# Value products and logits ahead of the output products behind the attention, and the last convolution on VectorE alone

## Chip, cores and metric

One core of a Trainium2 chip runs the whole program. The metric is device time in microseconds (us), the median of the runs shown. The profile is one further execution, and its times are counted from its first instruction.

## What is computed

The reference chains three blocks on 4 sequences of 576 rows (2304 rows, 512 channels). Cut to what matters:

```python
# 1 linear attention, 8 heads of 64, features exp(+-(x @ w_phi - max|x @ w_phi|))
num = einsum(q_p, einsum(k_p, v)); x = num / (einsum(q_p, sum(k_p)) + 1e-6)
# 2 gated convolution over the rows
gate = sigmoid(sum(conv_w[k] * shift(x, 4 - k) for k in range(5)))
y = (gate * (x @ w_val)) @ w_out
# 3 sticky top-1 mixture of 8 experts
logits = y @ w_gate; local = y @ w_local
e[s] = argmax(logits[s]) if s == 0 or sigmoid(local[s]) < 0.5 else e[s - 1]
out[s] = softmax(logits[s])[e[s]] * (relu(y[s] @ w1[e[s]]) @ w2[e[s]])
```

## The kernel before

The rows are cut into 18 tiles of 128 and 9 groups of 256. Each engine runs its instructions in the order in which the program has them. A scheduler sets that order from the order of the code and its own estimate of times; instructions given to `pin` (`keep_in_program_order`) keep the order of the code on their engine.

**Attention and mixing (to about 265 us).** `run` walks the k tiles and then the q tiles. For each finished group g, `push_mix` queues the work that follows: two pairs of value products (`val`, L356, tile `vps`, 24 products a pair, three for each fp32 product because both operands are split into a high and a low part), two tiles of output products of the group four back (`ypart`, `ymm`, L495, tile `yps`, 12 products a tile), and the logits (`lgt`, L395). `fill` takes from this queue between the attention's steps. `conv` (L228) makes the gate of a group, channel block by channel block (c = 0 to 3): one ScalarE product and four VectorE multiply-adds (`tap`, tile `acc`), then a tanh on ScalarE (`gp`). Block 3 is made on GpSimd instead (`pool`, L250, tile `p`). `val` ends in `gv = (gate + 1) * vps` on VectorE, which `need_gate` lets through when the gate's half is in `gated`; ScalarE casts it (`gh`) and GpSimd takes the rest (`gl`).

**Behind the attention.** The queue that is left (`vq`, L610 to L616) runs in its order: for groups 7 and 8 a pair of value products, a tile of output products, the other pair, another tile, then the logits. `lgt` multiplies `gv` by folded weights (`lpp`, 4 products, PSUM), ScalarE copies the result (`lpc`), PE adds it up (`lps`, 4 products) and VectorE copies it into `lg`. These tiles, `vps` and `yps` share three PSUM banks (`ps_b`). For the last group `probs` then chooses the experts and makes `code`.

**Routing (L628 to L720).** A chain of small steps alternates between VectorE and PE: transposes `tp`, `tc`, `tc`, `tb`, rank sums `rk`, then one-hot tables `ohc` (VectorE, ScalarE, GpSimd) and `ohl` (VectorE), and 18 products that add them into the slot table `tab`. From it VectorE makes the row indices `gidx` and `sidx`. Between the steps `yfill(n)` (L389) issues the next n output products of the tiles that are left (`rest`, L386), pinned. `yfill(99)` in front of `tab` issues all that remain. ScalarE evicts each finished tile into `ysb` and sends it to `y_d` in DRAM by DMA; GpSimd adds the probabilities to `ysb`.

**Experts (from about 330 us).** 8 units of 256 rows and 2 of 384. `gather` fetches rows of `y_d` by `gidx`, so it stands behind the last store to `y_d`. Expert weights come in pieces of 512 KB into three buffers `wraw` (L742); for each piece ScalarE casts the high part (`w1h`, `w2h`) and VectorE subtracts for the low part (`w1l`, `w2l`), both at helper lines L47 and L50. The four `w1` and four `w2` pieces of unit 0 are issued at L837 and the scheduler places them. PE makes `hp` (first layer) and `op` (second layer).

Of the kernel before, what the change touches and what calls it, by code (L numbers as in the profile page):

```python
# [14 lines left out]
ALU = mybir.AluOpType  # L15
# [15 lines left out]
YLAG = 4  # L31
# [4 lines left out]
def body(ctx, tc, qT, kT, v1, wbd, w_val, conv_w, w_out, w_gl, w1, w2, out):  # L36
# [184 lines left out]
    def bg(n, m=0):  # L221
        for i in range(n + m):
            if bgq and i < n:
                bgq.pop(0)()
            elif bg2 and len(done) == 4:
                bg2.pop(0)()

    def conv(g):  # L228

        x, cols, cw = xT[g], xcols(g), W["cw"]  # L230
        gp = mp.tile([128, 4, 256], F32, tag="gp", name="gp", bufs=2)
        gate_t[g] = gp
        last = g == NG - 1
        n = 256 + 4 * (len(cols) - 1)
        acc = {}

        def tap(c, kk):
            xs = x[:, c, kk:kk + n]
            if kk == 0:
                acc[c] = (ps_p if last else ps_c).tile([128, 512], F32, tag="pj" if last else "c", name="acc")[:, 0:n]  # L240
                A.activation(acc[c], xs, AF.Copy, scale=cw[:, kk, c:c + 1])  # L241
            else:
                V.scalar_tensor_tensor(acc[c], xs, cw[:, kk, c:c + 1], acc[c], ALU.mult, ALU.add)  # L243
            if kk == KC - 1:
                for off, m, fresh, col in cols:
                    A.activation(gp[:, c, off:off + m], acc[c][:, col - 4:col - 4 + m], AF.Tanh, scale=0.5)
                if c > 0:
                    gated.add((g, 2 * (c - 1)))

        def pool():  # L250

            o = mp.tile([128, 264], F32, tag="p0", name="p0", bufs=1)[:, 0:n]
            w = cw[:, :, 3:4]
            G.tensor_scalar(o, x[:, 3, 0:n], w[:, 0], None, op0=ALU.mult)
            for kk in range(1, KC):
                p = mp.tile([128, 264], F32, tag="p1", name="p1", bufs=1)[:, 0:n]
                G.tensor_scalar(p, x[:, 3, kk:kk + n], w[:, kk], None, op0=ALU.mult)
                G.tensor_tensor(o, o, p, ALU.add)
            for off, m, fresh, col in cols:
                A.activation(gp[:, 3, off:off + m], o[:, col - 4:col - 4 + m], AF.Tanh, scale=0.5)  # L260

        pool()
        for c in range(3):
            for kk in range(KC):
                if last:
                    tap(c, kk)
                elif kk == 0:
                    bgq.append(lambda c=c: (tap(c, 0), tap(c, 1)))
                elif kk > 1:
                    bgq.append(lambda c=c, kk=kk: tap(c, kk))  # L270
# [85 lines left out]
    def val(g, cp, ci):  # L356
        while len(done) < 4:
            bg(1)
        while len(odone) < min(g + 1, 4):
            bg2.pop(0)()  # L360
        vh, vl = W["val"]
        xh, xl = xs_t[g]
        if cp == 0 and ci == 0:
            gv_t[g] = mp.tile([128, 4, 256], F32, tag="gv", name="gv", bufs=2)
            g_t[g] = (mp.tile([128, 4, 256], F32R, tag="gh", name="gh", bufs=YLAG + 2),
                      mp.tile([128, 4, 256], F32R, tag="gl", name="gl", bufs=YLAG + 2))
        if ci == 0:
            W["vps"] = ps_b.tile([128, 2, 256], F32, tag="b", name="vps")
        vps = W["vps"]
        co = cp * 2 + ci  # L370
        n = 0
        for k in range(4):
            for wt, xt in ((vh, xh), (vl, xh), (vh, xl)):
                PE.matmul(vps[:, ci, :], lhsT=wt[:, k, co * 128:(co + 1) * 128], rhs=xt[:, k, :],
                          start=(n == 0 and ci == 0), stop=(n == 11 and ci == 1), skip_group_check=True)
                n += 1
        if ci == 1:
            sl = slice(cp * 2, cp * 2 + 2)
            gh, gl = g_t[g]
            need_gate(g, cp * 2)  # L380
            V.scalar_tensor_tensor(gv_t[g][:, sl, :], gate_t[g][:, sl, :], 1.0, vps, ALU.add, ALU.mult)
            hi_of(A, gh[:, sl, :], gv_t[g][:, sl, :])
            lo_of(G, gl[:, sl, :], gv_t[g][:, sl, :], gh[:, sl, :])

    p_t = {}
    rest = (mm for t in range(2 * (NG - YLAG), NT) for mm in ymm(t))  # L386
    pin = tc.keep_in_program_order

    def yfill(n):  # L389
        for _ in range(n):  # L390
            mm = next(rest, None)
            if mm is not None:
                pin(mm)

    def lgt(g):  # L395
        while bg2:
            bg2.pop(0)()
        if g == NG - 1:
            yfill(16)
        lpp = ps_b.tile([128, 256], F32, tag="b", name="lpp")  # L400
        for c in range(4):
            PE.matmul(lpp[32 * c:32 * c + 32, :], lhsT=W["l"][:, c, :], rhs=gv_t[g][:, c, :], start=True, stop=True,
                      skip_group_check=True)
        lpc = mp.tile([128, 256], F32, tag="lpc", name="lpc", bufs=2)
        A.copy(lpc, lpp)
        if g == NG - 1:
            yfill(5)
        lps = ps_b.tile([128, 2, E + 1], F32, tag="b", name="lps")
        for half in range(2):
            for mh in range(2):  # L410
                o = half * 128 + mh * 64
                mm = PE.matmul(lps[mh * 64:mh * 64 + 64, half, :], lhsT=lpc[:, o:o + 64], rhs=W["sel"],
                               start=(half == 0), stop=(half == 1), skip_group_check=True)
                if g == NG - 1:
                    pin(mm)
        V.tensor_copy(lg[:, 2 * g:2 * g + 2, :], lps)
        if g in ENDS:
            probs(ENDS[g], g + 1)
# [76 lines left out]
    def ymm(t):  # L495

        g, half = divmod(t, 2)
        gh, gl = g_t[g]
        oh, ol = W["out"]
        ts = slice(half * 128, half * 128 + 128)  # L500
        yps = ps_b.tile([128, 512], F32, tag="b", name="yps")
        for n in range(12):
            k, i = divmod(n, 3)
            gt, wt = ((gh, oh), (gh, ol), (gl, oh))[i]
            mm = PE.matmul(yps, lhsT=gt[:, k, ts], rhs=wt[:, k, :], start=(n == 0), stop=(n == 11))
            if n == 11:
                ysb = mp.tile([128, YW], F32, tag="ysb", name="ysb", bufs=3)
                A.activation(ysb[:, 0:D], yps, AF.Copy, scale=0.5)
                G.tensor_copy(ysb[:, D:YW], p_t[g][:, half, :])
                A.dma_start(y_d[t * 128:(t + 1) * 128, :], ysb)  # L510
            yield mm
# [3 lines left out]
    def ypart(t, part):  # L515
        if part == 0:
            ygen[t] = ymm(t)
        for _ in range(6):
            next(ygen[t])
# [4 lines left out]
    def push_mix(g):  # L524
        r = st["step"] + 2
        y0 = 2 * (g - YLAG)

        def q(c, f):
            fq.append((r, c, f))

        for cp in range(2):
            for ci in range(2):
                q(1.31, lambda cp=cp, ci=ci: val(g, cp, ci))
            if y0 >= 0:
                for part in range(2):
                    q(1.3, lambda cp=cp, part=part: ypart(y0 + cp, part))
        for z in ((), (0, 1))[g] if g < 2 else (g,):
            q(0.95, lambda z=z: lgt(z))

    def fill(budget):  # L540
        st["credit"] = min(st["credit"] + budget, 3.0)
        while fq and st["credit"] > 0 and fq[0][0] <= st["step"]:
            r, c, f = fq.pop(0)
            f()
            st["credit"] -= c

# [63 lines left out]
    vq = fq  # L610
    fq = []

    for item in vq:
        item[2]()
        bg(4)
    bg(1000)  # L616
    def t_(shape, nm, dt=F32):
        return r1.tile(shape, dt, name=nm)
# [32 lines left out]
    oh = ohp[:, :, 1:NT + 1]  # L651
    V.tensor_tensor(oh, ci.unsqueeze(1).to_broadcast([128, E, NT]), rc["w8i"].unsqueeze(2).to_broadcast([128, E, NT]), ALU.is_equal)
    rk = pst([128, E, NT + 1], "rk")
    yfill(5)
    pin(PE.matmul(rk[:, :, 0:NT], lhsT=rc["tri"], rhs=oh, start=True, stop=False, skip_group_check=True))

    def flat(a):
# [44 lines left out]
        pin(V.tensor_tensor(ohl[:, z, :], rc["io128"].unsqueeze(1).to_broadcast([128, HT, 128]),  # L702
                            lo[:, z].unsqueeze(2).to_broadcast([128, HT, 128]), ALU.is_equal))
    tab = pst([128, 2, NCOL], "tab")
    yfill(99)
    for t in range(NT):
        pin(PE.matmul(tab.rearrange("p a c -> p (a c)"), lhsT=ohl[:, t, :], rhs=ohc[:, t].rearrange("p a c -> p (a c)"),
                  start=(t == 0), stop=(t == NT - 1)))
    tk, tk2 = t_([128, NCOL], "tk"), t_([128, NCOL], "tk2")
    V.tensor_scalar(tk, tab[:, 0, :], 128.0, -128.0, op0=ALU.mult, op1=ALU.add)  # L710
    V.tensor_tensor(tk, tk, tab[:, 1, :], ALU.add)
# [122 lines left out]
        return i if i < E else eu_f[:, i - E:i - E + 1]  # L834

    cur_w, pieces = unit_weights(0)
    for p in pieces:  # L837
        p()()
    xs = gather(cols(gidx, units[0][0], units[0][1]))
    cur_x = rows(xs, unit_probs(0))  # L840
    for i, (c0, n, e) in enumerate(units):
# [68 lines left out]
```

## Time and profile before

| what | us |
|---|---|
| median of 3 runs | 612.9 |
| lowest and highest | 608.56, 613.07 |
| the profiled execution, own time | 611.88 |
| its span, first to last instruction | 610.1 |
| PE busy in the span | 573.3 |
| VectorE, ScalarE, GpSimd busy | 365.4, 298.3, 193.6 |

The profiled execution is 1.8 us longer than its span. In the rows, PE is TensorE, DVE is VectorE, ACT is ScalarE, POOL is GpSimd. A product's duration on PE overlaps the next one's, so the distance between two starts is what a product costs.

### The profile page before, as it was taken

The page shows a single profiled execution, that of the slowest core. Times are in us where ns is not written, and L with a number is a line of the kernel's source. Part 1 is how long each engine was busy: PE and PEld are TensorE (multiplying, and loading weights), DVE is VectorE, ACT ScalarE, POOL GpSimd, SP SyncE. Part 2 cuts the span into 40 slices and gives each one's busy share as a digit, 9 for nine tenths or more (in the row PEclk, how much of TensorE's full clock was granted, in tenths as well). Part 3 has the DMA queues.
Part 4 walks back from the last instruction along what each step waited for, and adds up shares of the span by engine and source line. Part 5 has one row for each costly group of instructions (what it writes and reads, how often), then busy time and mean ns, then how long its engine had stood idle before and what let it go on. Part 6 is the DMA issues. An engine that isn't in the chain of part 4 may idle for free. (4 is left out here: it accounts for less than half of the span.)

```text
span 610.1 us, 13253 instructions
## 1 busy us (share of the span) xinstructions
PE 573.3 (94%) x5376; PEld 495.7 (81%) x5376; DVE 365.4 (60%) x738; ACT 298.3 (49%) x545; POOL 193.6 (32%) x231
## 2 busy tenths in 40 slices
PE   7989999999999999988993999999998989999993
PEld 5767788898878888877773998989987879898982
DVE  5999867787877676584164676655654647451110
ACT  3657644465655554672224565555553636451210
POOL 2111100367766476495223202302302032011001
PEclk9999999999999999988996899999999989999997
DMA  9833422110010011033126877766866638530000
GB/s 286 315 104 102 113 72 70 37 36 27 28 37 18 20 52 39 19 122 139 52 89 211 257 227 241 267 196 211 261 190 224 213 116 248 197 96 34 17 17 36
DMA packets 46016, 76.81 MB, mean 126 GB/s; under 512 B 3839, under 2 KB 22399, under 8 KB 45952
## 3 DMA queue, kind: packets, MB, share of 16 engines
q1 hardware_dynamic: 39840, 60.55, 31.9%
q0 software_dynamic: 3520, 10.58, 4.8%
q10 hardware_dynamic: 2592, 4.79, 2.0%
q8 instruction: 44, 0.72, 0.5%
q14 instruction: 20, 0.16, 0.1%
HBM read 66.39 MB, written 10.56 MB: 126 GB/s over the span
## 5 line engine op out<-in xcount | busy, mean ns | idle before, releaser
L799 PE MATMUL hp<-xh,w1h 128*128 128x256 f32 (+1 forms) x320 | 95.8, 299 | 5.5 <-DVE hlo L802 4.8
L817 POOL DMA_INDIRECT out<-osb,sidx x22 | 29.9, 1358 | 207.2 <-ACT osb L816 164.4
L799 PE MATMUL hp<-xh,w1l 128*128 128x256 f32 (+1 forms) x320 | 95.3, 298 | 0.0
L799 PE MATMUL hp<-xl,w1h 128*128 128x256 f32 (+1 forms) x320 | 94.9, 298 | 0.0
L107 PE MATMUL pj<-wraw,raw 128*128 128x256 f32 x288 | 79.5, 407 | 7.7 <-DMA raw<-kT 3.6
L811 PE MATMUL op<-w2h,hh 128*128 128x512 f32 x176 | 69.0, 401 | 0.0
L799 PEld LDWEIGHTS hp<-xh,w1h 128*128 128x128 f32 x320 | 62.0, 194 | 8.0 <-DVE hlo L802 5.2
L811 PE MATMUL op<-w2l,hh 128*128 128x512 f32 x176 | 67.9, 395 | 0.0
L107 PEld LDWEIGHTS pj<-wraw,raw 128*128 128x128 f32 x288 | 51.4, 195 | 19.4 <-issue 4.3
L811 PE MATMUL op<-w2h,hlo 128*128 128x512 f32 x176 | 67.0, 396 | 0.0
L109 DVE TENSOR_REDUCE m<-pj 128x4 f32<-128x512 f32 x72 | 49.4, 686 | 25.9 <-PE pj L107 25.5
L799 PEld LDWEIGHTS hp<-xh,w1l 128*128 128x128 f32 x320 | 61.9, 193 | 1.6
L50 DVE TENSOR_TENSOR w2l<-wraw,w2h 128x1024 fp32r<-128x1024 f32 x40 | 48.8, 1225 | 22.7 <-ACT w2h L47 20.6
L50 DVE TENSOR_TENSOR w1l<-wraw,w1h 128x1024 fp32r<-128x1024 f32 x40 | 48.2, 1232 | 22.6 <-ACT w1h L47 22.5
L799 PEld LDWEIGHTS hp<-xl,w1h 128*128 128x128 f32 x320 | 61.6, 193 | 0.0
L802 DVE SCALAR_TENSOR_TENSOR hlo<-hp,hh 128x256 fp32r<-128x256 f32 (+1 forms) x80 | 34.2, 445 | 42.1 <-ACT hh L801 41.6
L243 DVE SCALAR_TENSOR_TENSOR acc<-xT,tfs,acc 128x256 f32<-128x256 f32 (+1 forms) x108 | 52.1, 487 | 9.9 <-ACT acc L241 8.7
L801 ACT ACTIVATE hh<-hp 128x256 fp32r<-128x256 f32 (+1 forms) x80 | 31.5, 404 | 51.9 <-PE hp L799 50.4
L47 ACT CAST w1h<-wraw 128x1024 fp32r<-128x1024 f32 x40 | 40.6, 1053 | 26.0 <-DMA wraw<-w 26.0
L47 ACT CAST w2h<-wraw 128x1024 fp32r<-128x1024 f32 x40 | 41.6, 1048 | 23.9 <-DMA wraw<-w 21.1
L111 DVE TENSOR_TENSOR pp<-pj,m 128x512 f32<-128x512 f32 x72 | 49.4, 685 | 4.4 <-PE tp L163 2.6
L136 PEld LDWEIGHTS kv<-v,ex 128*64 128x64 f32 (+1 forms) x1280 | 41.2, 137 | 12.2 <-issue 8.4
(180 smaller groups left out, 1176.2 us busy)
## 6 DMA issues: line engine op xcount, KB each, us to landing
wraw<-w SPq DMA_DIRECT2D x80, 512.0 KB, 4.3
v<-v SPq DMA_DIRECT2D x18, 260.0 KB, 4.4
y_d<-ysb ACTq DMA_DIRECT2D x18, 260.0 KB, 2.0
raw<-qT SPq DMA_DIRECT2D x18, 256.0 KB, 2.8
raw<-kT SPq DMA_DIRECT2D x17, 256.0 KB, 3.9
wr<-w_val SPq DMA_DIRECT2D x4, 512.0 KB, 5.9
wr<-w_out SPq DMA_DIRECT2D x4, 512.0 KB, 7.4
xg<-y_d,gidx POOLq DMA_INDIRECT x22, 5.6
```

Source lines behind the costliest of these rows:

```text
L47: (A.copy if eng is A else eng.tensor_copy)(hi, src)
L50: eng.tensor_tensor(lo, src, hi.bitcast(F32), ALU.subtract)
L107: PE.matmul(o, lhsT=raw[:, c, :], rhs=wraw, start=(cc == 0), stop=(cc == 1), skip_group_check=True)
L109: V.tensor_reduce(m, pj, axis=AX.X, op=ALU.max, apply_absolute_value=True)
L111: V.tensor_tensor(pp, pj, m.unsqueeze(2).to_broadcast([128, 4, 128]), ALU.subtract)
L136: PE.matmul(kv_ps[b][blk // 7][mh * 64:mh * 64 + 64, (blk % 7) * VW:(blk % 7 + 1) * VW], lhsT=kp_t[t, hh][off:off + n, sg, h, mh * 64:mh * ...
L243: V.scalar_tensor_tensor(acc[c], xs, cw[:, kk, c:c + 1], acc[c], ALU.mult, ALU.add)
L799: PE.matmul(hp[:, 0:n], lhsT=wt[:, k, f * 128:(f + 1) * 128], rhs=xt[:, k, 0:n], start=(i == 0), stop=(i == 11))
L801: A.activation(hh[:, f, 0:n], hp[:, 0:n], AF.Relu)
L802: V.scalar_tensor_tensor(hlo[:, f, 0:n], hp[:, 0:n], 0.0, hh[:, f, 0:n].bitcast(F32), ALU.max, ALU.subtract)
L811: PE.matmul(op, lhsT=ht[:, f, sl], rhs=wt[:, f, :], start=(i == 0), stop=(i == 23))
L817: G.indirect_dma_start(out=out, out_offset=bass.IndirectOffsetOnAxis(ap=scols[j], axis=0), in_=osb, in_offset=None, bounds_check=T - 1, oo ...
```

## The change

Four edits. (1) Behind the attention the output products of tiles above 5 (`need_y`) leave the queue and go to `rest`; the two pairs of value products of a group now follow each other. (2) `lgt` fills its own waits for groups 7 and 8 (6 products ahead of `lpp` of group 7, 16 ahead of that of group 8, 5 behind each), and in front of `tab` only 26 products stand; the last 60 follow behind `tab`. (3) For the last group block 3 of the gate is made like the others, on ScalarE and VectorE, and `pool` isn't called. (4) Unit 0's weight pieces get an order: their ScalarE instructions stand behind the last `lpc`, their VectorE instructions behind the last `gv`.

```diff
@@ conv
-                if c > 0:
-                    gated.add((g, 2 * (c - 1)))
+                if c == 1 or c == (3 if last else 2):
+                    gated.add((g, c // 2 * 2))
...
-        pool()
-        for c in range(3):
+        if not last:
+            pool()
+        for c in range(4 if last else 3):
@@ val
-            V.scalar_tensor_tensor(gv_t[g][:, sl, :], gate_t[g][:, sl, :], 1.0, vps, ALU.add, ALU.mult)
+            W["gv"] = V.scalar_tensor_tensor(gv_t[g][:, sl, :], gate_t[g][:, sl, :], 1.0, vps, ALU.add, ALU.mult)
@@ yfill, lgt
-    rest = (mm for t in range(2 * (NG - YLAG), NT) for mm in ymm(t))
+    rest = []
...
-        if g == NG - 1:
-            yfill(16)
+        if g >= NG - 2:
+            yfill((6, 16)[g - NG + 2])
...
-        A.copy(lpc, lpp)
-        if g == NG - 1:
+        W["lpc"] = A.copy(lpc, lpp)
+        if g >= NG - 2:
             yfill(5)
@@ behind run
+    need_y = 2 * (NG - 1 - YLAG - 2) + 1
+    rest += [ygen.get(t) or ymm(t) for t in range(max(need_y, max(ygen, default=0) - 1) + 1, NT)]
     for item in vq:
-        item[2]()
-        bg(4)
+        if item[3] is None or item[3] <= need_y:
+            item[2]()
+            bg(4)
@@ routing
-    yfill(5)
+    yfill(4)
     pin(PE.matmul(rk[:, :, 0:NT], lhsT=rc["tri"], rhs=oh, start=True, stop=False, skip_group_check=True))
...
-    yfill(99)
+    yfill(26)
     for t in range(NT):
         pin(PE.matmul(tab.rearrange("p a c -> p (a c)"), lhsT=ohl[:, t, :], rhs=ohc[:, t].rearrange("p a c -> p (a c)"),
                   start=(t == 0), stop=(t == NT - 1)))
+    yfill(999)
@@ unit 0
-    for p in pieces:
-        p()()
+    with tc.issue_after(W["gv"].ins), tc.issue_after(W["lpc"].ins):
+        for p in pieces:
+            p()()
```

Three places show how the engines' orders move. First VectorE behind the last `gv`, before (`lg` is the last group's logits, `code` its chosen experts, `sc` the first scan of the routing):

```order
L381 SCALAR_TENSOR_TENSOR gv<-gp,vps 128x512 x2
L416 COPY lg<-lps 128x18
L431 TENSOR_REDUCE mx<-lg 128x2
L491 SCALAR_TENSOR_TENSOR fr<-lg,s_115 128x2
L486 TENSOR_TENSOR eq<-lg,mx 128x16
L434 TENSOR_TENSOR pr<-lg,mx 128x16
L487 TENSOR_TENSOR eq<-eq,w_109 128x16
L489 TENSOR_REDUCE cc<-eq 128x2
L492 TENSOR_TENSOR cc<-cc,g_113 128x2
L493 TENSOR_TENSOR code<-cc,fr 128x2
```

The same place on VectorE in the changed kernel, in two pieces that follow each other:

```order
L382 SCALAR_TENSOR_TENSOR gv<-gp,vps 128x512 x2
L50 TENSOR_TENSOR w1l<-wraw,w1h 128x1024
L421 COPY lg<-lps 128x18
L50 TENSOR_TENSOR w1l<-wraw,w1h 128x1024
L436 TENSOR_REDUCE mx<-lg 128x2
L496 SCALAR_TENSOR_TENSOR fr<-lg,s_115 128x2
L50 TENSOR_TENSOR w1l<-wraw,w1h 128x1024
L491 TENSOR_TENSOR eq<-lg,mx 128x16
```

The second piece goes on to the first scan:

```order
L494 TENSOR_REDUCE cc<-eq 128x2
L497 TENSOR_TENSOR cc<-cc,g_113 128x2
L498 TENSOR_TENSOR code<-cc,fr 128x2
L50 TENSOR_TENSOR w1l<-wraw,w1h 128x1024
L442 TENSOR_REDUCE sm<-pr 128x2
L640 SCALAR_TENSOR_TENSOR sc<-onef,tp_4161 18x128
```

The four `w1l` of unit 0, which stood among the multiply-adds of the last convolution before, now stand between `gv` and `sc`: three ahead of `code`, the fourth ahead of `sc`.

ScalarE at the same place in the changed kernel (`pr` is the exponential of the last probabilities):

```order
L410 COPY lpc<-lpp 128x256
L47 CAST w1h<-wraw 128x1024 x3
L513 ACTIVATE ysb<-yps 128x512
L515 DMA y_d<-ysb 128x520
L47 CAST w1h<-wraw 128x1024
L440 ACTIVATE pr<-pr 128x16
```

Before, the last `lpc` was followed by an eviction and by `pr`; the four `w1h` stood ahead of it by two groups of value products, beside the last convolution.

TensorE behind the slot table, before (`xp` transposes the gathered rows of unit 0):

```order
L707 LDWEIGHTS ohl
L707 MATMUL tab<-ohc,ohl 128x80
L773 MATMUL xp<-ident,xg 128x128 x8
L799 MATMUL hp<-xh,w1h 128x256
L799 MATMUL hp<-xh,w1l 128x256
```

The same place in the changed kernel:

```order
L715 LDWEIGHTS ohl
L715 MATMUL tab<-ohc,ohl 128x80
L510 MATMUL yps<-wout_h,gh 128x512
L510 MATMUL yps<-wout_l,gh 128x512
L510 MATMUL yps<-wout_h,gl 128x512
```

Sixty output products, five tiles, now stand between the table and the first transposes. The total of output products is the same.

## Rows read from the trace of the kernel before

**Rows 1.** Windows: stretch, length, busy time of each engine, granted clock, DMA share, GB/s

```profile
270.00:290.00 20.00, 17.60 (x107) 15.46 (x107) 11.47 (x27) 7.71 (x15) 13.41 (x14) 0.87 0.38 133
...
310.00:320.00 10.00, 10.00 (x46) 8.00 (x45) 7.10 (x26) 3.47 (x6) 3.91 (x5) 1.00 0.22 82
```

**Rows 2.** Timeline, PE, groups 7 and 8: start, duration, instruction, [idle before, releaser]

```profile
267.27 0.41 PE L412 MATMUL lps<-sel,lpc 128*64 128x9 f32 x8 [1.60 <-ACT lpc L405]
267.60 0.39 PE L374 MATMUL vps<-xh,wval_h 128*128 128x256 f32 x1
...
272.08 0.39 PE L505 MATMUL yps<-wout_h,gh 128*128 128x512 f32 x1
...
274.86 0.27 PE L374 MATMUL vps<-xh,wval_h 128*128 128x256 f32 x1
...
277.72 0.40 PE L505 MATMUL yps<-wout_h,gh 128*128 128x512 f32 x1
...
280.57 0.64 PE L402 MATMUL lpp<-gv,wl 128*32 128x256 f32 x8
283.61 0.41 PE L412 MATMUL lps<-sel,lpc 128*64 128x9 f32 x8 [2.40 <-ACT lpc L405]
```

**Rows 3.** Timeline, ACT

```profile
274.95 1.05 ACT L47 CAST w1h<-wraw 128x1024 fp32r<-128x1024 f32 x1 [0.50 <-DMA wraw<-w]
...
282.39 0.42 ACT L260 ACTIVATE gp<-p 128x256 f32<-128x256 f32 x1 [2.84 <-POOL p L258]
...
301.33 0.37 ACT L405 COPY lpc<-lpp 128x256 f32<-128x256 f32 x1 [0.94 <-PE lpp L402]
```

**Rows 4.** Timeline, PE, last logits to the slot table

```profile
300.63 0.64 PE L402 MATMUL lpp<-gv,wl 128*32 128x256 f32 x8
...
302.55 0.41 PE L412 MATMUL lps<-sel,lpc 128*64 128x9 f32 x8
...
304.85 0.27 PE L630 MATMUL tp<-ident,code 128*18 128x128 f32 x1
...
305.98 0.17 PE L635 MATMUL tc<-ident,sc 18*1 18x18 f32 x1
...
310.49 0.48 PE L505 MATMUL yps<-wout_h,gh 128*128 128x512 f32 x1
...
321.44 0.39 PE L505 MATMUL yps<-wout_h,gl 128*128 128x512 f32 x1
321.67 0.82 PE L707 MATMUL tab<-ohc,ohl 128*128 128x80 bf16 x18
```

**Rows 5.** Timeline, DVE

```profile
262.88 2.06 DVE L243 SCALAR_TENSOR_TENSOR acc<-xT,tfs,acc 128x256 f32<-128x256 f32 x4
...
270.06 1.22 DVE L50 TENSOR_TENSOR w1l<-wraw,w1h 128x1024 fp32r<-128x1024 f32 x1
...
303.01 0.18 DVE L416 COPY lg<-lps 128x18 f32<-128x18 f32 x1 [8.05 <-PE lps L412]
...
304.24 0.16 DVE L493 TENSOR_TENSOR code<-cc,fr 128x2 f32<-128x2 f32 x1
...
305.16 0.41 DVE L632 TENSOR_TENSOR_SCAN sc<-onef,tp 18x128 f32<-18x128 f32 x1 [0.16 <-PE tp L630]
```

**Rows 6.** Timeline, POOL

```profile
315.41 3.52 POOL L700 TENSOR_TENSOR ohc<-ohc,tid 128x360 bf16<-128x360 bf16 x2 [5.28 <-ACT ohc L699]
...
325.50 1.46 POOL L761 DMA_INDIRECT xg<-y_d,gidx  x1 [6.32 <-ACT w2h L47]
```

**Rows 7.** Weight loads of L747 issued from 262 to 345 us

```profile
DMA to landing us min/median/max: 3.4/4.5/5.9
```

**Rows 8.** Timeline, PE, a gap in the expert stage

```profile
470.79 0.39 PE L799 MATMUL hp<-xh,w1h 128*128 128x256 f32 x1 [2.24 <-DVE hlo L802]
```

**Rows 9.** Windows behind two gaps of PE, columns as in rows 1

```profile
287.00:288.00 1.00, 1.00 (x7) 1.00 (x6) 0.00 (x0) 0.00 (x0) 0.00 (x0) 0.50 0.00 0
470.00:472.00 2.00, 1.21 (x10) 1.21 (x11) 1.16 (x4) 0.00 (x0) 0.00 (x0) 1.00 0.00 0
```

More of the change, by code (lines that the diff above doesn't have):

```diff
@@ L390, in yfill @@
         for _ in range(n):
-            mm = next(rest, None)
-            if mm is not None:
-                pin(mm)
+            while rest:
+                mm = next(rest[0], None)
+                if mm is None:
+                    rest.pop(0)
+                else:
+                    pin(mm)
+                    break
     def lgt(g):
@@ L413, in lgt @@
                                start=(half == 0), stop=(half == 1), skip_group_check=True)
-                if g == NG - 1:
+                if g >= NG - 2:
                     pin(mm)
@@ L526, in push_mix, with q @@
         y0 = 2 * (g - YLAG)
-        def q(c, f):
-            fq.append((r, c, f))
+        def q(c, f, y=None):
+            fq.append((r, c, f, y))
         for cp in range(2):
@@ L535, in push_mix @@
                 for part in range(2):
-                    q(1.3, lambda cp=cp, part=part: ypart(y0 + cp, part))
+                    q(1.3, lambda cp=cp, part=part: ypart(y0 + cp, part), y0 + cp)
         for z in ((), (0, 1))[g] if g < 2 else (g,):
@@ L542, in fill @@
         while fq and st["credit"] > 0 and fq[0][0] <= st["step"]:
-            r, c, f = fq.pop(0)
+            c, f = fq.pop(0)[1:3]
             f()
```

## The prediction

> **What bounds the kernel now.** I read the windows first, to find the stretch that the change touches. From 310 to 320 us PE is busy all the time at full clock, and from 270 to 290 us it is busy for 17.60 of 20 us at a mean clock of 0.87 [rows 1]. So behind the attention TensorE sets the pace, and what the change can win is PE's idle time and the clock that follows it. Then PE's timeline for groups 7 and 8 [rows 2]. It has two gaps, both in front of `lps` and both ended by ScalarE's `lpc`: 1.60 us at 267.27 and 2.40 us at 283.61. Behind the first, 24 value products take 272.08 - 267.60 = 4.48 us; undisturbed, 24 take 277.72 - 274.86 = 2.86 us. The difference, 1.6 us, is what one fall of the clock costs. ScalarE's timeline names the second gap's cause: `gp` waits 2.84 us for GpSimd's `p`, the last gate block, and `lpc` stands behind it in ScalarE's order [rows 3]. Last, PE from the last logits to the table [rows 4]: no gap at all. From 310.49 to 321.44 us there are 48 output products, 47 steps, 0.23 us each.
>
> I call L the start of the last `lpp`, 300.63 us before [rows 4], and count the routing from it.
>
> **Edits 1 and 3, up to L: a gain.** The first gap stays: the order up to 267.60 us is the same on PE. From there the changed order has 96 value products (24 still in the low clock 4.48, 72 at full clock 3 x 2.86 = 8.58), 27 output products (6 + 5 + 16, 27 x 0.23 = 6.2) and one `lpp` and `lps` (283.61 - 280.57 less the gap of 2.40, and 0.34 to the next product: 1.0) [rows 2]. The fourth convolution block adds four multiply-adds on VectorE, 2.06 us [rows 5], ahead of the second `gv` of group 7. They lie beside the second pair of value products; only if they come late does `lpp` wait, between 0 and 1.0 us, and I take 0.2. That is 20.4 us, so L is 288.0 instead of 300.63. Of these 12.6 us, 37 products (8.5 us) are only moved behind L. The rest, about 4 us, is the second gap (2.40) and its fall of the clock (1.6). GpSimd's convolution leaves the chain, so nothing late replaces it: `lpc` of group 7 now waits for `gv` and `lpp`, some 0.5 us before five output products have run.
>
> **Edit 4, behind L: a loss.** The weight pieces left the convolution's stretch and landed in the routing chain. In the changed order `w1h` follows `lpc` on ScalarE, and VectorE has a `w1l` ahead of `lg`, a second ahead of `mx`, a third ahead of `eq`, a fourth ahead of `sc`. What is queued behind the first `w1l` is the whole routing, and PE waits for it at `tp`. `lpc` ends 1.07 us behind L [rows 3]; a `w1h` takes 1.05 [rows 3] and a `w1l` 1.22 [rows 5]. So the first `w1l` starts at L + 2.15 and three of them take 3.66; from `lg` to the end of `code` is 304.40 - 303.01 = 1.39 [rows 5]. `code` is ready at L + 7.2. PE stands ready earlier: `lps` at L + 1.92 as before [rows 4], 0.34 for it, 8 products 1.84, so L + 4.1. `tp` runs at L + 7.3 instead of L + 4.22, behind a gap of 3.2 us.
>
> The fourth piece needs a `wraw` buffer, which the first `w1l` frees at L + 3.4. Its load before took from the end of the first `w1l` (271.28 [rows 5]) to 274.95 [rows 3], 3.67 us; loads here take 3.4 to 5.9 [rows 7]. With 3.67, cast and subtraction `sc` starts at L + 9.35, takes 0.41, and `tc` runs at L + 9.85 instead of L + 5.35: 4.5 us later, with a second gap of about 1.6 us. The bounds for the load move this by -0.3 and +2.2 us.
>
> **Edit 2, the table.** From `tc` to the product behind `rk` were 310.49 - 305.98 = 4.5 us [rows 4]; one product fewer stands there, so L + 14.1. From there the table's operands took until 315.41 + 3.52 = 318.93, 8.4 us [rows 6], all on VectorE, ScalarE and GpSimd and none of it shorter now. Before, 48 products covered it and `tab` came at 321.67 with nothing waiting. Now 26 products, 6.0 us, stand there, and PE waits about 2.4 us; half of the table's 18 products can run inside that. `tab` is done at L + 23.0. The 60 products behind it take 13.8, the last one's own end 0.15: L + 36.95, or 324.95 us. Before, the last output product ended at 321.83 [rows 4]. That is 3.1 us later.
>
> The gather doesn't profit from the early table. It reads `y_d`, so it stands behind the last store, and that behind the eviction of the last product. It began at 325.50 [rows 6], 3.67 us behind the last product. That tail is the same in the new order. Before, the table's 0.82 us lay inside this tail; now it lies in front of the products. The expert stage has nearly the same order and I cost it at nothing.
>
> **The clock.** Behind the gap of 2.40 us PE runs at 0.50 (1.2 GHz) [rows 9]; behind a gap of 2.24 us in the expert stage [rows 8] it stays at 1.00 (2.4 GHz) [rows 9]. So a gap brings a fall often, not always. New are gaps of 3.2, 1.6 and about 2.4 us, the first two close together and with products on the path behind them. Bounds: no fall 0, three falls 3 x 1.6 = 4.8. I take 3.0, nearer the upper end: both gaps of [rows 2] were followed by a slow stretch, the one at 470 wasn't.
>
> The Trainium skill, "TensorE: Matmul & The Clock Gate", section "Part 1: The HAM clock gate (the "warmup" mystery)", says that how many products run cold varies from run to run of one kernel. By that rule the number of falls isn't fixed by the gaps, which is the second rival's case; here one gap with a fall and one without agree with it.
>
> The same page, section "Back-to-back issue gap", gives 216 ns for a product of 512 columns where the rows give 0.23 us. By the page the 60 products would be an estimated 13.0 us and the sum 0.8 us less; the measured step decides.
>
> **Sum.** 611.88 (the profiled execution's own time) + 3.1 + 3.0 = 618.0. The median of the runs shown is 1.0 above that execution and their spread is 4.5, so I leave the sum as it is. About 1% (6.1 us) is what a measurement of this kernel can tell from no change; the forecast lies just inside it, on the slow side.
>
> **Rivals.** (a) The split isn't in the way: the casts run before `lg` is ready. Then `tc` comes at L + 5.35 and the last product ends 4.5 us earlier, at 320.45; with one fall at the table's gap (1.6) that is 0.2 above before, 612.1, and without it 610.5, so not slower. If the table's wait is covered too (2.4) it is 608.1, and with the two gaps of the expert stage smaller it could pass 1%. For it: VectorE idles 8.05 us ahead of `lg` [rows 5], so there is room. Against it: the order puts `w1h` behind `lpc`, and the point from which it decides is whether three `w1h` end before L + 2. They can't if ScalarE starts them at L + 1.07. (b) All waits come as computed but the clock holds: 611.88 + 3.1 = 615.0. For it, the window at 470 [rows 9]; against it, the gap at `tp` is 1 us longer than the one that kept the clock [rows 8]. (c) The fourth load lands late (5.9 instead of 3.67, +2.2) and all three falls come (+1.8 over mine): 622.0. For it, three loads queue together behind the split; against it, the DMA engines are little used there (0.22 [rows 1]).
>
> **How the numbers follow.** The forecast 0.52, (b) 0.20, (a) 0.18, (c) 0.10. The forecast's own range is 616 to 620. The range 611.5 to 622.5 takes in (b), (c) and the upper half of (a). Slower by over 1% (above 619.0): a little over half of the forecast's upper part, 0.28, and (c), 0.10: 0.38. Faster by over 1% (below 606.8): a third of (a), 0.06. Within 1%: 0.56.
>
> **What would show it.** In the changed profile `lps` of group 7 has no idle time ahead of it and the last `lpp` starts near 288. PE has a gap of about 3 us ahead of `tp`, ended by VectorE's `code`, one ahead of the first `tc`, ended by `sc`, and one ahead of `tab`, ended by GpSimd's `ohc`. VectorE's idle time ahead of the first `w1l` is ended by `w1h`, and ScalarE's ahead of the fourth `w1h` by its load. The last output product ends near 325 to 328 us. The forecast is wrong if PE has no gap ahead of `tp`, if `w1l` is done before `lg`, or if the gather begins at 322 us or earlier.

## The result and the profile after

The changed kernel took 620.89 us, the median of 4 runs (617.36 to 622.03), beside 611.75 for the kernel before (4 runs, 608.56 to 613.07). The ratio is 1.0146, with a 95% interval of 1.0107 to 1.0184: slower, inside the predicted range and 2.9 us above the 618.0 of the forecast. Timed again later in six more runs it took 618.49 (614.95 to 621.86) beside 612.44, a ratio of 1.0117 [1.0071, 1.0163]. As a difference, the forecast was 6.1 us, and the two timings gave 9.1 and 6.1. Ratios, here and below, leave out runs that are over 1.5% above the fastest of their kernel.

PE's timeline of the changed kernel, from the logits of group 7 to the experts (start, duration, instruction, idle time before it and what ended that); the rows of before are [rows 2, 4 and 8]:

```profile
278.63 0.41 PE L417 MATMUL lps<-sel,lpc 128*64 128x9 f32 x8
...
288.58 0.64 PE L407 MATMUL lpp<-gv,wl 128*32 128x256 f32 x8
...
295.32 0.28 PE L638 MATMUL tp<-ident,code 128*18 128x128 f32 x1 [2.36 <-DVE code L498]
...
298.29 0.19 PE L643 MATMUL tc<-ident,sc 18*1 18x18 f32 x1 [1.76 <-DVE sm L443]
...
305.80 0.78 PE L510 MATMUL yps<-wout_l,gh 128*128 128x512 f32 x1
...
313.40 0.48 PE L715 MATMUL tab<-ohc,ohl 128*128 128x80 bf16 x9 [0.95 <-POOL ohc L708]
314.15 0.48 PE L715 MATMUL tab<-ohc,ohl 128*128 128x80 bf16 x9 [0.27 <-POOL ohc L708]
314.46 0.47 PE L510 MATMUL yps<-wout_h,gh 128*128 128x512 f32 x1
...
328.17 0.40 PE L510 MATMUL yps<-wout_h,gl 128*128 128x512 f32 x1
...
340.29 0.58 PE L808 MATMUL hp<-xh,w1h 128*128 128x256 f32 x1 [0.67 <-ACT xh L47]
...
477.33 0.57 PE L808 MATMUL hp<-xh,w1h 128*128 128x256 f32 x1 [2.13 <-DVE hlo L811]
...
506.86 0.38 PE L808 MATMUL hp<-xh,w1h 128*128 128x256 f32 x1 [3.93 <-DVE hlo L811]
```

The 2.40 us ahead of `lps` of group 7 [rows 2] are gone, and the last `lpp` (L) starts 12 us earlier than at 300.63 [rows 4]. Behind it stand two gaps that weren't there, 2.36 us ahead of `tp` and 1.76 ahead of `tc` (which reads `sc`; the row names `sm`, the step behind it on VectorE), and 1.2 us of waiting at the table. The last output product starts at 328.17 where it started at 321.44 [rows 4]. VectorE and ScalarE of the same stretch say what PE waited for; VectorE's last three rows are from the expert stage:

```profile
290.64 1.23 DVE L50 TENSOR_TENSOR w1l<-wraw,w1h 128x1024 fp32r<-128x1024 f32 x1 [4.95 <-ACT w1h L47]
291.79 0.17 DVE L421 COPY lg<-lps 128x18 f32<-128x18 f32 x1
291.87 1.22 DVE L50 TENSOR_TENSOR w1l<-wraw,w1h 128x1024 fp32r<-128x1024 f32 x1
...
293.15 1.22 DVE L50 TENSOR_TENSOR w1l<-wraw,w1h 128x1024 fp32r<-128x1024 f32 x1
...
295.10 0.16 DVE L498 TENSOR_TENSOR code<-cc,fr 128x2 f32<-128x2 f32 x1
296.62 1.23 DVE L50 TENSOR_TENSOR w1l<-wraw,w1h 128x1024 fp32r<-128x1024 f32 x1 [1.35 <-ACT w1h L47]
...
297.84 0.40 DVE L640 TENSOR_TENSOR_SCAN sc<-onef,tp 18x128 f32<-18x128 f32 x1
...
498.97 0.42 DVE L811 SCALAR_TENSOR_TENSOR hlo<-hp,hh 128x256 fp32r<-128x256 f32 x1
505.27 0.17 DVE L792 TENSOR_TENSOR es<-es,xg 128x8 f32<-128x8 f32 x1 [5.88 <-DMA xg<-y_d,gidx]
...
506.39 1.08 DVE L811 SCALAR_TENSOR_TENSOR hlo<-hp,hh 128x256 fp32r<-128x256 f32 x3
```

```profile
289.56 2.95 ACT L47 CAST w1h<-wraw 128x1024 fp32r<-128x1024 f32 x3
...
295.54 1.05 ACT L47 CAST w1h<-wraw 128x1024 fp32r<-128x1024 f32 x1 [2.54 <-DMA wraw<-w]
```

`lg` comes directly behind `lps` [rows 5], but here a subtraction of 1.2 us stands ahead of each of `lg`, `mx`, `eq` and `sc`, and the first starts only when ScalarE's first cast is done. The fourth cast waits for its load. The windows of the same stretch (length, busy time of each engine, granted clock, DMA share, GB/s) show the clock:

```profile
294.00:298.00 4.00, 1.22 (x5) 0.69 (x5) 2.54 (x10) 1.16 (x2) 0.35 (x1) 0.81 1.00 377
298.00:302.00 4.00, 3.71 (x10) 2.48 (x10) 1.15 (x7) 0.60 (x1) 0.00 (x0) 0.50 0.49 176
302.00:306.00 4.00, 4.00 (x12) 2.21 (x11) 0.98 (x3) 0.00 (x0) 0.19 (x1) 0.50 0.17 67
306.00:310.00 4.00, 4.00 (x18) 3.25 (x18) 3.80 (x24) 0.88 (x2) 0.00 (x0) 0.91 0.18 69
312.00:330.00 18.00, 15.35 (x80) 11.98 (x79) 1.85 (x8) 3.94 (x7) 2.93 (x7) 1.00 0.20 75
```

PE works all the time from 302 to 306 us, but at 0.50 (1.2 GHz): 12 instructions in 4 us, where 18 go through in the next 4, at 0.91. The waits at the table bring no fall: 1.00 (2.4 GHz) from 312 to 330. GpSimd's timeline closes the stretch: the table's last operand, and the first gather 3.67 us behind the last product's end (328.57), as before.

```profile
311.45 2.65 POOL L708 TENSOR_TENSOR ohc<-ohc,tid 128x360 bf16<-128x360 bf16 x2 [7.88 <-ACT ohc L707]
...
332.24 1.98 POOL L770 DMA_INDIRECT xg<-y_d,gidx  x1 [8.92 <-DVE w2l L50]
```

### The profile page after: what moved, and what is told of

The parts are those of the page before. It is cut to its first block, busy times and chain, and to the rows that moved or that the text cites. A ratio compares the mean times of both kernels' runs of the same rounds, so it can differ in the third digit from the quotient of the medians.

```text
span 620.2 us, 13251 instructions
## 1 busy us (share of the span) xinstructions
PE 577.5 (93%) x5376; PEld 496.9 (80%) x5376; DVE 364.8 (59%) x742; ACT 297.9 (48%) x546; POOL 183.1 (30%) x222
## 5 line engine op out<-in xcount | busy, mean ns | idle before, releaser
L826 POOL DMA_INDIRECT out<-osb,sidx x22 | 28.1, 1276 | 211.2 <-ACT osb L825 167.8
L243 DVE SCALAR_TENSOR_TENSOR acc<-xT,tfs,acc 128x256 f32<-128x256 f32 (+1 forms) x112 | 53.4, 487 | 9.8 <-ACT acc L241 8.7
```

What stands on the lines that cost most here:

```text
L826: G.indirect_dma_start(out=out, out_offset=bass.IndirectOffsetOnAxis(ap=scols[j], axis=0), in_=osb, in_offset=None, bounds_check=T - 1, oo ...
```

## The experiments

My theory was that the loss is edit 4: the split in the routing chain leaves PE idle ahead of `tp` and `tc`, and the clock falls behind the gaps. Against it stood that the table's wait and the 60 products behind it cost the time; that the chain's lateness itself sets the end; and that the expert stage got slower. In what follows a kernel's "tail" is the time from L to the start of its last output product: 20.81 us before, with 37 products fewer in it and the table behind it, and 39.59 after.

**Parts of the change.** First the changed kernel without edit 4:

```diff
-    with tc.issue_after(W["gv"].ins), tc.issue_after(W["lpc"].ins):
-        for p in pieces:
-            p()()
+    for p in pieces:
+        p()()
```

> The changed kernel without edit 4: unit 0's four casts and subtractions stand again beside the last convolution, everything else as changed. Theory A (the weight split in the routing chain costs the time): no wait of PE ahead of tp (2.36 us) and the first tc (1.76 us), one fall of the clock fewer (1.6 us), so the last output product ends near 322 to 323 us instead of 328.6 and the time is 5 to 6 us below the changed kernel, 614 to 616. Theory B (the 60 products behind the slot table cost it): both waits may go, but the time stays within 2 us of the changed kernel, 619 to 621. Theory C (the expert stage alone differs, by 3.8 us in the two profiles): within 2 us of the changed kernel up to the last product, and the difference sits behind 340 us.

Measured: 610.93 us, ratio to before 1.0013 [0.9977, 1.0049]. PE has no gap from `lps` of group 7 to the table, the tail is 321.21 - 289.44 = 31.77 us, and the whole loss is gone. That is 3 us below theory A's range: the tail is 7.8 us shorter, where A had counted 5.7 for the two gaps and one fall of 1.6. The wait at the table (1.38 us) and the 60 products behind it stay in this kernel, so they aren't the loss.

Then edit 4 with the split kept in order, but behind the table's operands and `sidx`:

```diff
-    with tc.issue_after(W["gv"].ins), tc.issue_after(W["lpc"].ins):
+    with tc.issue_after(W["sx"].ins), tc.issue_after(W["oc"].ins):
```

> The changed kernel with edit 4's order put later: the ScalarE casts of unit 0's first-layer weights behind the last ohc, the VectorE subtractions behind sidx, beside the 60 products. Theory A: both waits go as in e1, and the last convolution is free of the split too, so the last product ends near 321 to 322 us, 613 to 615 in all; the unit's first hp isn't late, since the split (four times 1.2 us and one load of 3.7) fits into the 14 us of the 60 products. Theory B: 619 to 621. A rival to A within it: the split becomes late for hp, then PE waits for w1l behind the gather and the time stays near 618.

Measured: 611.12, ratio 1.0006 [0.9969, 1.0044]; tail 318.66 - 286.87 = 31.79; again under theory A's range. So it isn't that the pieces have an order, but where that puts them. Next, edit 3 alone in the kernel before (the diff's part under `conv`):

> The kernel before with edit 3 alone: the last convolution's block 3 on ScalarE and VectorE. Expected from the gap of 2.40 us ahead of lps of group 7, which stood behind GpSimd's last block: the gap and its fall of the clock (1.6 us) go, the last product ends near 318 us and the time is 608 to 609, 3 to 4 us below before. Rival: VectorE, which then has 2.06 us more beside the four w1l, makes gv of group 7 late and PE waits for it instead; then 611 to 613.

Measured: 609.95, ratio 0.9994 [0.9952, 1.0036]. The gap ahead of `lps` of group 7 is 0.49 us, no half clock follows, and the last output product starts at 318.15, 3.3 us earlier. The time lies between the range given for the gain and the rival's, and no gain can be told from the timed runs. And edit 4 alone in the kernel before:

```diff
+            W["gv"] = V.scalar_tensor_tensor(gv_t[g][:, sl, :], gate_t[g][:, sl, :], 1.0, vps, ALU.add, ALU.mult)
...
+        W["lpc"] = A.copy(lpc, lpp)
...
+    with tc.issue_after(W["gv"].ins), tc.issue_after(W["lpc"].ins):
```

> The kernel before with edit 4 alone: unit 0's casts behind the last lpc and its subtractions behind the last gv, the output products where they were. Theory A: PE waits ahead of tp and tc, 2.4 and 1.8 us as in the changed kernel, and the clock falls behind them once (1.6), 5.8 us; against that GpSimd's last block no longer shares its time with w1l (1.8 to 2.0 us an operation beside it, 0.9 without) and ends about 3 us earlier, which takes the gap of 2.40 us and its fall away (4.0). Sum about 2 us above before, 613 to 615. Theory B: this kernel has no product behind the table, so it isn't slower than before, 608 to 612.

Measured: 613.94, ratio 1.0054 [1.0014, 1.0094]. The gaps ahead of `tp` (2.35) and `tc` (2.02) appear here too, with half clock (0.50) in both windows from 306 to 314 us and 0.82 in the next, and the tail grows from 20.81 to 326.20 - 297.20 = 29.00. But the gap ahead of `lps` of group 7 shrinks to 0.49 as well, though the convolution is still on GpSimd. GpSimd's groups from 262 to 286 us say why (busy time, mean ns of one, idle time before); in the kernel before, with `w1l` beside it on VectorE:

```profile
L257 POOL TENSOR_SCALAR p<-xT,tfs 128x256 f32<-128x256 f32 x6 | 7.3, 1216 | 0.5
L258 POOL TENSOR_TENSOR p<-p,p 128x256 f32<-128x256 f32 x7 | 6.1, 873 | 0.3
...
L254 POOL TENSOR_SCALAR p<-xT,tfs 128x256 f32<-128x256 f32 x1 | 2.0, 1987 | 0.0
```

And with edit 4 alone, where the subtractions have left this stretch:

```profile
L257 POOL TENSOR_SCALAR p<-xT,tfs 128x256 f32<-128x256 f32 x6 | 5.5, 925 | 0.4
L258 POOL TENSOR_TENSOR p<-p,p 128x256 f32<-128x256 f32 x7 | 5.2, 739 | 0.3
...
L254 POOL TENSOR_SCALAR p<-xT,tfs 128x256 f32<-128x256 f32 x1 | 0.9, 922 | 0.0
```

The same instructions take less time: the first product 1987 - 922 = 1065 ns less, a little under one subtraction (1.22 us). The Trainium skill, "SBUF — State Buffer", section "SBUF: two separate sides", says that VectorE, in an instruction with two inputs in SBUF, and GpSimd lock a shared pair of ports, and that the one that comes second is blocked for the whole instruction; these rows agree, since `w1l` has two such inputs. In the kernel before, the four long instructions of GpSimd (1.99, 1.73, 1.83 and 1.78 us) each ran beside one of the four `w1l`. ScalarE's casts, which edit 4 moved too, aren't the cause: one runs from 269.36 us beside a multiply of the usual 0.93.

```profile
269.10 0.93 POOL L257 TENSOR_SCALAR p<-xT,tfs 128x256 f32<-128x256 f32 x1
270.00 1.99 POOL L254 TENSOR_SCALAR p<-xT,tfs 128x256 f32<-128x256 f32 x1
272.07 1.73 POOL L258 TENSOR_TENSOR p<-p,p 128x256 f32<-128x256 f32 x1
...
269.36 1.04 ACT L47 CAST w1h<-wraw 128x1024 fp32r<-128x1024 f32 x1
...
271.98 1.22 DVE L50 TENSOR_TENSOR w1l<-wraw,w1h 128x1024 fp32r<-128x1024 f32 x1
```

The gap that I put down to the slow GpSimd convolution was there because VectorE's split ran beside it. Edits 3 and 4 remove the same gap, each alone.

**Idle time or lateness?** The split stays in the chain, but PE gets products to do while it waits:

```diff
-    yfill(8)
+    yfill(20)
     pin(PE.transpose(tp, rc["code"], ident))
...
-    yfill(4)
+    yfill(13)
     pin(PE.transpose(tc1, sc[:, 127:128], ident[0:NT, 0:NT]))
```

> The changed kernel with the weight split where it is, but 20 output products ahead of tp instead of 8 and 13 ahead of the first tc instead of 4; 39 instead of 60 then follow the table. Theory A (the loss is PE's idle time ahead of tp and tc, 2.36 + 1.76 us, and the half clock that followed it, about 3.6 us): tp and tc come as late as in the changed kernel (295.3 and 298.3 within 0.5), without a gap, no half clock behind tc, the last output product ends about 7.5 us earlier, near 321, and the time is 612 to 614.5. Rival B (the routing chain's lateness itself sets the end, by the table, the indices or unit 0's weights): the last product comes early but the gather or the first hp waits for sidx, gidx or w1l, and the time stays at 618 to 622. Rival C (the clock falls on its own account): no gap, half clock all the same, 616 to 618.

Measured: 610.58, ratio 0.9999 [0.9957, 1.0042], 1.4 us below theory A's range. PE's timeline and a window of this kernel:

```profile
286.87 0.64 PE L407 MATMUL lpp<-gv,wl 128*32 128x256 f32 x8
...
293.86 0.27 PE L638 MATMUL tp<-ident,code 128*18 128x128 f32 x1
...
297.07 0.17 PE L643 MATMUL tc<-ident,sc 18*1 18x18 f32 x1
...
318.68 0.40 PE L510 MATMUL yps<-wout_h,gl 128*128 128x512 f32 x1
```

```profile
298.00:302.00 4.00, 4.00 (x19) 2.48 (x18) 1.78 (x8) 0.60 (x1) 0.38 (x2) 1.00 0.70 255
```

`tp` comes at L + 6.99 and `tc` at L + 10.20, later than in the changed kernel (6.74 and 9.71). Yet there is no gap, the clock stays at 1.00, and the tail is 31.81, as with no split in the way. The lateness of the chain costs nothing here; PE's idle time and the half clock behind it were the loss. (Counted from the start of the span, `tp` came 1.4 us before the 295.3 that I expected: L is 1.7 us earlier, most of it because of an earlier fall of the clock that this execution doesn't have; it comes up again under "Twice the same kernel".)

Then only three pieces in the chain, the fourth and the `w2` pieces behind the table:

```diff
     with tc.issue_after(W["gv"].ins), tc.issue_after(W["lpc"].ins):
-        for p in pieces:
+        for p in pieces[:3]:
+            p()()
+    with tc.issue_after(W["sx"].ins), tc.issue_after(W["oc"].ins):
+        for p in pieces[3:]:
             p()()
```

> The changed kernel with three of unit 0's w1 pieces in the routing chain, and the fourth and the w2 pieces behind the slot table. Theory A: the gap ahead of tp stays (2.1 to 2.6 us, ended by DVE code), that ahead of tc (1.76) goes, since sc no longer stands behind the fourth w1l, which waited for its load. If the one gap brings the half clock, 618 to 619.5; if it takes both gaps, 614.5 to 616. Rival (the ACT casts of the first three hold lpc, pr or ysb, and both gaps come from them): the gap ahead of tc stays, 620 to 622.

Measured: 616.83 over all ten runs (610.82 to 620.17) and 615.73 over the eight of the ratio, which is 1.0064 [1.0021, 1.0108]. The profiled execution took 618.13. PE and a window of it:

```profile
293.93 0.28 PE L638 MATMUL tp<-ident,code 128*18 128x128 f32 x1 [2.36 <-DVE code L498]
...
295.35 0.18 PE L643 MATMUL tc<-ident,sc 18*1 18x18 f32 x1
```

```profile
294.00:298.00 4.00, 4.00 (x12) 2.37 (x13) 1.06 (x6) 0.43 (x1) 0.19 (x1) 0.58 0.81 299
```

The gap ahead of `tc` is gone, as the theory has it, and half clock follows the one gap, but only within this window: 0.99 in the next. The tail is 322.91 - 287.20 = 35.71, that is 3.9 above 31.81: the gap of 2.36 and 1.5 for the fall, the size that [rows 2] gave. For a half clock behind the one gap I had given 618 to 619.5; the profiled execution lies there, the median doesn't. I had counted down from the 620.89; on the 611 of the versions without the loss, 3.9 makes 615.

**Twice the same kernel.** The changed kernel's expert stage, from the first `hp` to the end of the span, took 620.2 - 340.29 = 279.9 us, beside 610.1 - 334.00 = 276.1 before. Is that the change?

> The changed kernel unaltered, a second profile. If the 3.8 us that its expert stage was longer than before (from the first hp to the end: 279.9 against 276.1) belong to the change, 279.5 to 280.3 again, with the gaps at the same two units. If the length varies from run to run with the gaps ahead of hp and the half clock behind them, another length by 1 us or more, anywhere between 273 and 281. The gaps ahead of tp and tc come again within 0.2 us either way; the half clock behind them by theory A again.

Measured: 614.5 us for this one execution; 612.8 - 337.46 = 275.3 us for the stage. The tail is 37.63, with gaps of 2.35 and 0.83, the second not within the 0.2 of 1.76 that I expected. One more thing differs: the gap of 1.60 us ahead of `lps` of group 6 [rows 2], which every profile here has, is followed by half clock in the first profile of this kernel and not in this one.

```profile
268.00:276.00 8.00, 8.00 (x52) 7.87 (x53) 6.80 (x18) 2.95 (x8) 2.57 (x3) 0.79 0.28 110
```

```profile
268.00:276.00 8.00, 8.00 (x68) 7.23 (x68) 7.60 (x19) 3.63 (x10) 2.85 (x3) 1.00 0.30 113
```

Between the same two instructions, from this `lps` to the last `lpp`, PE took 21.04 us in the first and 19.84 in the second.

> The changed kernel unaltered, timed in more rounds, since one further execution took 614.5 us, below the four of the first comparison (617.36 to 622.03). Theory A with a clock that falls in some executions more than in others: a spread of 612 to 623, a median of 616 to 620, 0.8 to 1.4% slower than before. If the first four stand for all: 620 to 622.

Measured: 618.49 (614.95 to 621.86), ratio 1.0117 [1.0071, 1.0163]. The profiled execution has a stage of 275.8, a tail of 38.02 and gaps of 2.36 and 1.42. The first four runs were on the high side.

> The kernel before unaltered, a second profile. If the expert stage's length belongs to the kernel, from first hp to the end 276.1 within 0.5 again; if it varies from run to run, another by 1 us or more, with other sizes of the gaps ahead of hp. The gap of 2.40 us ahead of lps of group 7 comes again within 0.2.

Measured: 614.44 us for this execution of the kernel before. The gap ahead of `lps` of group 7 is 2.40 again, but this time no half clock follows: the clock from 284 to 290 us is 1.00, where the first profile has 0.72.

```profile
284.00:290.00 6.00, 6.00 (x41) 5.50 (x41) 2.55 (x14) 1.17 (x3) 1.63 (x3) 1.00 0.12 45
```

The stage takes 612.7 - 333.23 = 279.5, and its two longest gaps are

```profile
469.96 0.58 PE L799 MATMUL hp<-xh,w1h 128*128 128x256 f32 x1 [2.43 <-DVE hlo L802]
...
499.89 0.39 PE L799 MATMUL hp<-xh,w1h 128*128 128x256 f32 x1 [4.42 <-DVE hlo L802]
```

where [rows 8] and a gap of 2.56 stood. So the stage differs between executions of one kernel, by 3.4 us here and by 4.6 in the changed kernel, and there is no sign that the 3.8 us that it was longer in the changed kernel's profile are the change's.

**Versions that might beat both.** The split behind the table, and 36 products ahead of the table so that it needn't wait:

```diff
-    yfill(26)
+    yfill(36)
     for t in range(NT):
```

> The changed kernel with unit 0's whole weight split behind the slot table, and 36 instead of 26 output products in front of the table (50 behind). The wait ahead of the table's second half (1.38 us, ended by GpSimd's ohc, with 26) goes. If PE's idle time is what counts, 1.4 us less than with 26: 609.0 to 610.2. Rival (that wait is given back in the expert stage, as 3.3 us of the last convolution's gain were): 610.7 to 611.5. That rows of products ahead of the table make the gather later: 612 or more.

Measured: 609.39, ratio 0.9995 [0.9956, 1.0034]. The table waits for nothing and the tail is 30.11, 1.7 shorter, but against before no gain can be told.

The gaps of the expert stage have a cause that VectorE's rows above show: `hlo` at 506.39 stands behind `es`, which waits 5.88 us for gathered rows that only a later unit needs, and PE waits for `hlo` (506.86, 3.93 us). So the two steps that read a probability from the rows are put behind the split of these rows, on top of the last version:

```diff
-            lo_of(V, xl[:, :, sl], xp, xh[:, :, sl])
+            xi = lo_of(V, xl[:, :, sl], xp, xh[:, :, sl])
...
-                V.tensor_copy(p, xg[:, D + probs:D + probs + 1])
+                with tc.issue_after(xi.ins):
+                    V.tensor_copy(p, xg[:, D + probs:D + probs + 1])
...
-                V.tensor_tensor(es, es, xg[:, D:YW], ALU.mult)
-                V.tensor_reduce(p, es, axis=AX.X, op=ALU.add)
+                with tc.issue_after(xi.ins):
+                    V.tensor_tensor(es, es, xg[:, D:YW], ALU.mult)
+                    V.tensor_reduce(p, es, axis=AX.X, op=ALU.add)
```

> The kernel with the split behind the table and 36 products ahead of it, and in the expert stage the two steps that read a probability from a gathered row (es, p) ordered on VectorE directly behind xl of the same rows, instead of ahead of hlo. Theory D (the gaps of PE ahead of hp that VectorE's hlo ends, 1.33 + 1.91 us in that kernel's profile, 2.1 to 3.9 each in the changed kernel's, come from es, which waits for the gathered rows and has hlo queued behind it): those gaps go under 0.5 us each, the stretch from the first hp to the end falls from 275.3 to 271 to 273, and the time is 605.5 to 608. Rival (the rows themselves are late, and the wait only moves to the transposes xp or to xl): gaps of the same sum under another name, 609 to 611.

Measured: 605.93 (603.58 to 608.94), ratio 0.9902 [0.9867, 0.9937]: faster than both kernels. No gap ahead of an `hp` is ended by `hlo` any more. The stage takes 606.0 - 332.13 = 273.9, 1.4 less than in the version without it and 0.9 above the upper end that I gave. Its window from 460 to 520 us:

```profile
460.00:520.00 60.00, 59.87 (x392) 53.85 (x391) 36.28 (x60) 31.44 (x53) 15.69 (x11) 1.00 0.71 224
```

The same window of the changed kernel:

```profile
460.00:520.00 60.00, 53.94 (x330) 48.65 (x329) 30.60 (x52) 29.25 (x46) 11.46 (x9) 0.94 0.59 186
```

That is 392 products in 60 us instead of 330, though not the same ones: the fastest version is 8 us further on in its stage there. And that one edit in the kernel before:

> The kernel before, with that one edit of the expert stage alone (es and p behind xl). Theory D: the gaps of 2.24 and 2.56 us ahead of hp go, first hp to end 276.1 becomes 272 to 274, time 2 to 4 us under that of before, 607 to 609. Rival (the rows are late): 610.5 to 612.

Measured: 608.63, ratio 0.9948 [0.9917, 0.9978]; stage 608.2 - 335.93 = 272.3; no gap of PE ahead of an `hp` is ended by `hlo`. (The gap ahead of `lps` of group 7 is 3.89 us in this profile: no half clock follows the gap of 1.60, so PE comes to its wait 1.35 us earlier, and `lps` starts at 283.75 where it was 283.61.) The rows weren't late for PE, only for VectorE's order.

## Why the prediction was right

The direction, the place and the mechanism held: PE idles ahead of `tp` and `tc` behind the weight split, and the clock falls there. That the price came out so close is in part luck, as the steps show. From the profiled execution of 622.03 us:

- **Up to L.** 288.0 was predicted and 288.58 came (286.87 to 289.44 in the kernels that share these edits). The sum has one fall behind the gap of 1.60 in it; it came in this profile and not in the two later ones of the same kernel, whose L is 287.66 and 287.30. The gap ahead of `lps` of group 7 went, and nothing late replaced it. The cause was only half right: not GpSimd's convolution as such, but that convolution beside VectorE's split.
- **`tp` and `tc`.** `code` at L + 7.2 and `tc` at L + 9.85 were predicted; L + 6.7 and L + 9.71 came. The gap at `tp` is 2.36 instead of 3.2: PE was ready at L + 4.4 instead of 4.1, and three subtractions take 1.14 us from start to start of the next step, not 1.22. The fourth load took 3.67 us (291.87 to 295.54), the value taken. It did so although the DMA engines weren't little used: the 0.22 that I held against rival (c) is from 310 to 320 us of the kernel before, and the DMA share of the changed kernel is 1.00 from 294 to 298.
- **The clock.** Predicted: 3.0 for the new gaps. The product behind `rk`, put at L + 14.1 without the clock, came at L + 17.22, 3.1 later. The price was right for this profile, its split was not: I had added falls of 1.6 us each and counted the table's gap as a possible cause too. What came is one stretch at half clock, about 10 us long by the windows above, and no profile shows a fall at the table.
- **The table.** 2.4 us of waiting were predicted; 0.95 + 0.27 came here, 1.38 in most of the other kernels. But what enters the sum is the time from the product behind `rk` to the first product behind the table, and that was nearly right: 8.9 predicted, 314.46 - 305.80 = 8.66 measured. GpSimd's last operand took 2.65 us where I had 3.52 from [rows 6], but it started later, and its end came 8.30 us behind that product instead of 8.4; PE's wait was shorter because the 26 products, some of them at half clock, took longer than 6.0.
- **The products behind it.** 13.8 predicted, 328.17 - 314.46 = 13.71 for 59 steps, 0.23 each. The last one starts at L + 39.59, against L + 36.8 and 3.0 for the clock. The tail to the gather is 3.67 again.
- **The expert stage, costed at nothing.** In this profile it is 3.8 longer, and that is nearly all of what the profiled execution is above the forecast (622.03 - 618.0 = 4.0); the other runs behind the median of 620.89 have no profile. Over three profiles of the changed kernel it is 279.9, 275.3 and 275.8, over two of before 276.1 and 279.5. As a mean, nothing is a fair price; what was missing is that it varies by over 4 us, with waits for `hlo` that both kernels have.

Rival (a), that the split isn't in the way, fell with the gap at `tp`. Rival (b), that the clock holds, fell with the windows from 298 to 306 us. Rival (c), a load of 5.9 us and three falls, didn't come: the load took 3.67 us, the table brought no fall, and the profiled execution came to 622.03 by its expert stage. The prediction gave 0.38 to a loss of over 1% and 0.56 to less; both ratios lie over 1%, the second with an interval that reaches below it.

The Trainium skill, "TensorE: Matmul & The Clock Gate", section "Part 1: The HAM clock gate (the "warmup" mystery)", says that the number of cold products varies from run to run. The profiles agree: of the fourteen here, all with the gap of 1.60 us ahead of `lps` of group 6, half clock follows it in eight and not in six. Behind the gaps at `tp` and `tc` the price differs too: with the tail of 31.81 and the two gaps taken off, the fall cost 39.59 - 31.81 - 4.12 = 3.7 us in one profile of the changed kernel, 37.63 - 31.81 - 3.18 = 2.6 and 38.02 - 31.81 - 3.78 = 2.4 in the others.

Edits 1 to 3 without the loss (610.93, 611.12) can't be told from before, though they take a gap and its fall away. The prediction's own sum for this, rival (a) without a fall, was 610.5: the table's wait and its products now stand in front of the last products and take back most of the gain. What stays open is what makes the clock fall behind one gap and not behind another of the same size, and why the first gathered rows came to PE 6.75 us after the gather's start in the fastest version (329.04 - 322.29) where it was 5.01 in the version that it builds on (327.65 - 322.64).

## What to carry to other kernels

When work is moved off a crowded stretch, look at what is queued behind it on each engine in its new place: 1.2 us of subtraction are nothing on an idle VectorE and everything ahead of a step that TensorE waits for. Where a chain must be late, give TensorE work in front of its waiting instruction; in the run that did so the same lateness cost nothing, and the clock didn't fall. An instruction that waits for a DMA and whose result isn't needed soon belongs behind the work that is, even if it is tiny.

## What the runs showed of the hardware

That GpSimd's multiplies of 128x256 fp32 take 1216 ns on average with VectorE's subtractions of 128x1024 among them, and 925 without, was not in my reckoning, which had looked at each engine by itself. A gap of PE of 2.36 us was followed by half clock in every profile that has it ahead of `tp`, one of 1.38 ahead of the table in none. But a gap's length doesn't settle it: 2.40 us ahead of `lps` of group 7 was followed by half clock in one profile of the kernel before and not in the other, 1.60 in eight of fourteen profiles, and a gap of 3.50 us ahead of an `hp`, in the profile of the version with three pieces in the chain, wasn't.

```profile
504.70 0.39 PE L808 MATMUL hp<-xh,w1h 128*128 128x256 f32 x1 [3.50 <-DVE hlo L811]
...
506.00:512.00 6.00, 6.00 (x29) 4.92 (x28) 4.52 (x5) 3.71 (x5) 0.00 (x0) 1.00 0.25 63
```

The half clock lasted longer where a second gap followed: with gaps of 2.36 and 1.76 it fills the two windows from 298 to 306 us and reaches into both beside them, with the first gap alone it stays inside one.
